# Spectral filter and gated feed-forward on one core: the constant-term column's products in a bank of their own, and three small moves around it

## The chip, the cores and the metric

The kernel runs on one core of a Trainium2 chip. The metric is device time in microseconds for one execution. The profile is one execution, recorded by the hardware profiler; its span runs from the first to the last instruction.

The core has five engines that run side by side and wait for each other by semaphores: TensorE (PE; its weight loads are listed apart as PEld), VectorE (DVE), ScalarE (ACT), GpSimd (POOL) and SyncE (SP), which here only issues DMAs. Each engine runs its own instructions in the order in which the program gives them.

## What is computed

The reference, cut to what matters (`x` is 8192 tokens of 448 channels; `sa`, `ca`, `ga`, `sb`, `cb`, `gb` are six rows made from a condition vector):

```python
h = layernorm(x) * (1 + ca) + sa
Xf = rfft2(h, axes=(tokens))                 # complex, per channel
z = Xf.reshape(..., 4, 112)                  # four blocks of channels
hr = relu(zr @ w1[0] - zi @ w1[1] + b1[0])
hi = relu(zi @ w1[0] + zr @ w1[1] + b1[1])
or_ = softshrink(hr @ w2[0] - hi @ w2[1] + b2[0], 0.01)
oi_ = softshrink(hi @ w2[0] + hr @ w2[1] + b2[1], 0.01)
x = x + ga * irfft2(or_ + 1j * oi_)
h = layernorm(x) * (1 + cb) + sb
x = x + gb * ((gelu(h @ w_gate) * (h @ w_up)) @ w_down)
```

All the edits lie in the first half, the spectral filter.

## The kernel before

**Stages.** The Fourier transform over 8192 tokens is split into two: a first transform over 128 (`dft_a`, with the layer norm's scales folded into its matrix), written to DRAM (`td`), and a second over 64 with the twiddles in its matrices. Then follow the complex two-layer perceptron per frequency, the inverse of the second transform (`stage_i1`), a store to DRAM (`vd`), and, in the second half of the kernel, the inverse of the first. After that the feed-forward part runs over 32 chunks of 256 tokens, and takes the rest of the time; nothing of the change is in it.

**Units and steps.** The frequencies are worked on in 32 units: 16 groups `bt` of four first-transform frequencies, times two halves `h` of the channels (two blocks of 112 each, `kk` 0 and 1). The order of the groups is 1, 2, 3, 4, 0, 5, ..., so the two units of group 0 are units 8 and 9. `step(i)` is a software pipeline written out by hand. In this order it

- fetches unit i+2 from `td` (`fetch_t`, L417, on SP's queue),
- runs the second transform of unit i (`stage_s2`): products L449, L450 and L455 into two banks tagged `pa`, then per block a cast on ScalarE (`zh`, L461) and a residual on VectorE (`zl`, L462),
- splits unit i+1 into a high and a low part (`split_t`: L115 and L117, on POOL; for the first two units on ScalarE and VectorE),
- runs the second layer of unit i-2 (`stage_m2`): products L522 to L529 into a bank tagged `pc`, twice (`p` 0 and 1); ScalarE's L538 and four VectorE instructions L546 apply the threshold and write `y`,
- runs the first layer of unit i-1 (`stage_m1`): 12 products per block (L494 to L501) into a bank tagged `pb`, then ScalarE's `hh` (L508) and VectorE's `hl` (L509),
- splits `y` (`yh` on ScalarE, `yl` on POOL), and
- runs the inverse of unit i-3 (`stage_i1`): L575 to L577 into two banks tagged `pd`, copied out by ScalarE as `us` (L579) and stored.

Each tag has two banks, used in turn: a tile waits until the last reader of the tile before the last has finished. The `pd` banks also serve the weight norms (`pw`, L809, emptied by VectorE's L816) and, for group 0, `pn`.

Between these stages `step` calls hooks (`"load"`, `"pe"`, `"pool"`, `"act"`, `"dve"`), to which `at(i, hook, fn)` pins other work, such as weight norms (`squares` L798 or L800, `norms` L809), sums of the third weight (L937 to L941) and its maxima (L925). A list `tiny` holds small instructions; each call of `drip()` (two in a transform, four in a second layer, two in a first layer) issues the next one. `VL` and `SL` put VectorE and ScalarE instructions on this list.

**The constant term.** The frequency 0 of group 0 and the Nyquist frequency are both real, and share one complex column (column 0). For group 0, `stage_s2` therefore copies the imaginary part of column 0, the Nyquist value, to an extra column (L470) and clears what has to be zero (L468, L469, L471), on POOL. `stage_m1` runs the first layer on two extra columns: 12 more products of two columns per block, behind the 12 main ones, into columns 448 and up of the bank that the second layer of the same step has just used (`last["pm2"]`). Column 0 then gets its constant from VectorE (L512 to L514). `stage_m2` runs the second layer for the extra columns (`pn`), and VectorE's L555 and L557 add the result to `y`.

**The start.** Before step 0 the modulation columns and rows are computed and folded into the first layer's weights. The two halves of `wt`, one per layer, lie in one tile of the pool `lp`, which is closed before the steps begin. The second layer's weights are scaled by `col2`, cast (`weights2_hi`: ScalarE's L320), and their residual and the negated copies made (`weights2_lo`: VectorE's L324 twice, POOL's L328 and L329 twice each). `row_copy` copies two rows (`sb_r`, `cb_r`) out of two `pd` banks.

**Row scales.** At the end of step 13 `row_scales` puts on the list `tiny`: two maxima on VectorE, four small VectorE instructions that make the scale `sk`, and two ScalarE instructions that scale `sb_r` and `cb_r` by it (all shown at L604).

Of the kernel before, what the change touches and what calls it, by code (L numbers as in the profile page):

```python
# [10 lines left out]
F32 = mybir.dt.float32  # L11
# [39 lines left out]
def spectral_geglu(ctx, tc, x, w1, b1, w2, b2, wg, wu, wd, cvec, wmod, cf1, cs2, cmi, cgm, out):  # L51
# [92 lines left out]
    with ExitStack() as actx:  # L144
# [8 lines left out]
        wt = lp.tile([113, 2, 2, NBLK, BS], F32, name="wt")  # L153
# [104 lines left out]
        col2 = lp.tile([113, 1], F32, name="col2")  # L258
# [9 lines left out]
        def dc_cols():  # L268

            ps = bank("pc", "psd")  # L270
            for r in range(2):
                for k in range(NBLK):
                    T.matmul(ps[:112, 4 * r + k : 4 * r + k + 1], wt[:112, 0, r, k, :], sa0[:, k : k + 1], start=True, stop=True)
            return lambda: V.tensor_scalar(hb, ps[:112, : 2 * NBLK], wsc[:112, 0:1], None, op0=ALU.mult)
# [22 lines left out]
        def modulated():  # L297
            V.tensor_tensor(
                w1m, wt[:, 0], ca1.rearrange("p (r k o) -> p r k o", r=1, o=1).to_broadcast([113, 2, NBLK, BS]), ALU.mult
# [17 lines left out]
        def weights2_hi():  # L317
            V.tensor_tensor(col2, col2, wsc[:113, 1:2], ALU.mult)
            wr = wt[:, 1].rearrange("p r k o -> p k r o")
            S.activation(wv[0][:, 0], wr, AF.Copy, scale=col2)  # L320

        def weights2_lo():
            for r in range(2):
                V.scalar_tensor_tensor(  # L324
                    wv[1][:, 0, :, r], wt[:, 1, r], col2, wv[0][:, 0, :, r], op0=ALU.mult, op1=ALU.subtract
# [12 lines left out]
        def load_mlp():  # L338
            for l, (w, b) in enumerate(((w1, b1), (w2, b2))):
                for r in range(2):  # L340
                    dma(wt[:112, l, r], w[r].rearrange("k i o -> i k o"))
                    dma(wt[112:113, l, r], b[r : r + 1])
            dma(mi, cmi)

        def mlp_bounds():
# [3 lines left out]
            for l in range(2):  # L349
                V.tensor_reduce(  # L350
                    wmx[:, l : l + 1], wt[:, l].rearrange("p r k o -> p (r k o)"), mybir.AxisListType.X, ALU.max, apply_absolute_value=True
# [55 lines left out]
    with ExitStack() as bctx:  # L407
# [31 lines left out]
        def stage_s2(h, bt):  # L439
# [11 lines left out]
            for kk in range(2):  # L451
# [13 lines left out]
                if bt == 0:  # L465

                    for z in (zhi, zlo):
                        G.memset(z[:BS, 0, ZW - 1 : ZW], 0.0)  # L468
                        G.memset(z[:BS, 1, ZW - 2 : ZW], 0.0)  # L469
# [6 lines left out]
        last = {}  # L476

        def stage_m1(h, bt):
            zs = ctx_u.pop(("z", h, bt))
            hs = []  # L480
            w = GB * 64
            for kk in range(2):
                k = 2 * h + kk
                zhi, zlo = zs[kk]
                ps = bank("pb", "pm1")
                outs = [(ps[:BS, : 2 * w], 0, w)]
                if bt == 0:
                    outs.append((last["pm2"][:BS, D + 4 * kk : D + 4 * kk + 4], w, 2))
                for e, c0, n in outs:
                    q = slice(c0, c0 + n)  # L490
                    o = [e[:, ro * n : (ro + 1) * n] for ro in range(2)]
                    for ro in range(2):
                        a, c = (0, 2) if ro == 0 else (1, 0)
                        T.matmul(o[ro], w1h[:113, a, k, :], zhi[:113, 0, q], start=ro == 0, stop=False)  # L494
                        T.matmul(o[ro], w1l[:113, a, k, :], zhi[:113, 0, q], start=False, stop=False)  # L495
                        T.matmul(o[ro], w1h[:BS, c, k, :], zhi[:BS, 1, q], start=False, stop=False)  # L496
                        T.matmul(o[ro], w1l[:BS, c, k, :], zhi[:BS, 1, q], start=False, stop=False)  # L497
                    for ro in range(2):
                        a, c = (0, 2) if ro == 0 else (1, 0)
                        T.matmul(o[ro], w1h[:BS, a, k, :], zlo[:, 0, q], start=False, stop=False)  # L500
                        T.matmul(o[ro], w1h[:BS, c, k, :], zlo[:, 1, q], start=False, stop=ro == 1)  # L501
                hhi = hh_[cnt["h"] % 4]
                cnt["h"] += 1
                hlo = bp.tile([BS, 2, ZW], F16, tag="hl", name="hl", bufs=4)
                for e, c0, n in outs:
                    q = slice(c0, c0 + n)
                    pv = e.rearrange("p (r q) -> p r q", r=2)
# [1528 lines left out]
```

## Time and profile before

| | |
|---|---|
| time, median of 3 runs | 1875.99 us (1871.98 to 1878.42) |
| the profiled execution | 1877.36 us, span 1875.3 us |
| TensorE matmuls busy | 1830.7 us, 98% of the span, 23400 instructions |
| VectorE busy | 1410.3 us, 75% |
| ScalarE busy | 973.3 us, 52% |
| GpSimd busy | 1313.4 us, 70% |
| mean granted TensorE clock | 0.987 of full |
| the steps of the spectral filter | from 79 us on; units 8 and 9 pass their first layers in the steps begun at 141.45 and about 156 us |

A row of a timeline gives the start in us from the span's start, the duration, the engine, the line of the kernel, the operation, output and inputs by name, and in brackets how long the engine stood idle before it and what ended the wait. Rows that belong together are merged (x2 is two instructions). A matmul's end is modelled, and matmuls overlap, so that their spacing is read from their starts. A window gives the busy time of each engine in a stretch, the TensorE clock that was granted (1.00 is full, 0.50 half), the mean share of the DMA engines' time in use, and GB/s moved.

### The profile page before, as it was taken

The numbers are of one execution on the slowest core, as the hardware profiler recorded it, in microseconds if no ns is written. First come the engines' busy times: TensorE is split into PE (matmuls) and PEld (weight loads), VectorE is DVE, ScalarE is ACT, GpSimd is POOL, SyncE is SP. The second block draws the span as 40 slices with busy tenths as digits, with TensorE's granted clock in tenths as the row PEclk, the third lists the DMA queues.
The fourth block names the chain that finished last, engine by engine and source line by source line (L and its number), as shares of the span: only waits on it lengthen the run. The fifth ranks groups of instructions, "written<-read, shape, count | busy, mean of one in ns | idle before, by whom it ended". The sixth has DMA issues, their size and how long they took to land.

```text
span 1875.3 us, 56506 instructions
## 1 busy us (share of the span) xinstructions
PE 1830.7 (98%) x23400; PEld 1737.4 (93%) x23400; DVE 1410.3 (75%) x2898; ACT 973.3 (52%) x1821; POOL 1313.4 (70%) x1721
## 2 busy tenths in 40 slices
PE   7999999899999999999999999999999999999998
PEld 3698889778899898999999999999999999999998
DVE  8786899887766667777777777777777777777745
ACT  5675678653444444455555555555555554444443
POOL 3475778347777778777777777777777777777534
PEclk9997999999999999999999999999999999999999
DMA  9887767664444445966666666666666676666661
GB/s 354 302 288 232 220 193 224 195 175 100 117 104 103 104 88 124 304 170 171 169 170 169 169 169 169 170 171 177 177 176 170 173 178 176 176 174 177 152 164 55
DMA packets 380089, 330.48 MB, mean 176 GB/s; under 512 B 110260, under 2 KB 358200, under 8 KB 379832
## 3 DMA queue, kind: packets, MB, share of 16 engines
q1 hardware_dynamic: 379832, 326.87, 63.2%
q8 instruction: 183, 3.00, 0.7%
q14 instruction: 74, 0.61, 0.1%
HBM read 243.32 MB, written 60.10 MB: 162 GB/s over the span
## 4 chain that ended last, share of the span: by engine, by line
PE 87%; DVE 5%; DMA 4%; ACT 2%; SPq 1%; issue 1%; POOL 1%; ACTq 0%; DVEq 0%; POOLq 0%
PE set L1471 39%; PE pgu L1228 10%; PE pdn L1301 6%; PE pdn L1303 6%; PE pdn L1302 6%; PE set L1302 2%; PE set L1303 2%; PE set L1301 2%; PE ps L213 2%; DMA xt<-in_A_x 2%; DVE y L546 1%; PE pm L494 1%; PE pm L496 1%; PE pm L495 1%; PE pm L497 1%
## 5 line engine op out<-in xcount | busy, mean ns | idle before, releaser
L1471 PE MATMUL set<-nt,wk 128*128 128x128 f16 x13104 | 736.6, 219 | 2.2 <-DMA wk<-wk 1.0
L1471 PEld LDWEIGHTS <-wk 128*128 128x128 f16 x13104 | 733.9, 98 | 2.8 <-issue 1.6
L1303 PE MATMUL pdn<-wd,ac 128*128 128x224 f16 x1218 | 315.5, 259 | 0.6 <-DVE ac L1289 0.6
L1301 PE MATMUL pdn<-wd,ac 128*128 128x224 f16 x1218 | 315.7, 259 | 0.0
L1302 PE MATMUL pdn<-wd,ac 128*128 128x224 f16 x1218 | 315.5, 259 | 0.0
L1228 PE MATMUL pgu<-nt,wk 128*128 128x256 f16 (+1 forms) x2464 | 268.0, 273 | 3.2 <-DVE x L1269 3.1
L1228 PEld LDWEIGHTS <-wk 128*128 128x128 f16 (+1 forms) x2464 | 225.6, 98 | 44.3 <-issue 18.7
L1520 ACT ACTIVATE gl<-c,dg 128x384 f32<-128x384 f32 x168 | 103.5, 616 | 230.6 <-DVE c L1514 227.7
L1546 DVE SCALAR_TENSOR_TENSOR ac<-x,sa_act,ac 128x896 f16<-128x896 f32 x168 | 206.3, 1228 | 20.2 <-ACT ac L1536 20.2
L1277 POOL TENSOR_TENSOR x<-x 128x128 f32<-128x128 f32 x223 | 131.6, 590 | 118.1 <-DVE x L1269 57.5
L1347 POOL TENSOR_TENSOR cq<-cq 128x224 f32<-128x224 f32 x32 | 21.1, 659 | 261.7 <-DVE cq L1346 261.7
L1278 POOL TENSOR_TENSOR x<-x 128x128 f32<-128x128 f32 x223 | 185.0, 830 | 17.5
L1536 ACT ACTIVATE ac<-x,sa_act 128x896 f16<-128x896 f32 x168 | 174.2, 1037 | 14.5 <-POOL x L1280 7.8
L1524 DVE TENSOR_TENSOR x<-c,gl 128x384 f32<-128x384 f32 x168 | 153.2, 912 | 17.2 <-ACT gl L1520 17.1
L1301 PEld LDWEIGHTS <-ac 128*128 128x128 f16 x1568 | 153.4, 98 | 4.9 <-issue 4.8
L1303 PEld LDWEIGHTS <-ac 128*128 128x128 f16 x1568 | 153.4, 98 | 0.8 <-DVE ac L1289 0.8
L1302 PEld LDWEIGHTS <-ac 128*128 128x128 f16 x1568 | 153.5, 98 | 0.1
L1508 DVE TENSOR_TENSOR c<-set,sb 128x512 f32<-128x512 f32 x168 | 115.4, 687 | 36.1 <-PE set L1471 36.0
L117 POOL TENSOR_TENSOR yl<-y,yh 128x448 fp32r<-128x448 f32 x63 | 87.2, 1400 | 68.7 <-ACT yh L115 51.0
L1279 POOL TENSOR_TENSOR x<-x 128x128 f32<-128x128 f32 x223 | 132.9, 596 | 0.0
L1264 ACT ACTIVATE gel<-pgu,dg 128x256 f32<-128x256 f32 x112 | 49.5, 471 | 156.9 <-PE pgu L1228 149.3
L1499 ACT COPY sb<-set 128x512 f32<-128x512 f32 x168 | 97.6, 581 | 61.3 <-PE set L1471 60.0
(330 smaller groups left out, 3869.1 us busy)
## 6 DMA issues: line engine op xcount, KB each, us to landing
wk<-wk SPq DMA_DIRECT2D x76, 1024.0 KB, 8.9
wk<-wk SPq DMA_DIRECT2D x76, 768.0 KB, 5.1
tr<-td SPq DMA_DIRECT2D x32, 448.0 KB, 4.8
vd<-us SPq DMA_DIRECT2D x64, 224.0 KB, 3.2
xx<-in_A_x SPq DMA_DIRECT2D x32, 448.0 KB, 4.8
v<-vd SPq DMA_DIRECT2D x63, 224.0 KB, 5.6
out<-x SPq DMA_DIRECT2D x31, 448.0 KB, 6.4
xt<-in_A_x SPq DMA_DIRECT2D x15, 896.0 KB, 14.8
```

The source lines that it names most:

```text
L1228: T.matmul(pgu[i, t, q][:, pr * H : (pr + 1) * H], ws[rows, n, w, tw], nts[i][rows, tn, :], start=start, stop=stop, skip_group_check=True,)
L1277: e.tensor_tensor(s1, a21, a22, ALU.add)
L1278: e.tensor_tensor(s2, s1, a11, ALU.subtract)
L1279: e.tensor_tensor(s3, a11, a21, ALU.subtract)
L1301: T.matmul(ps, ac[:, 0, ka], w[:, 0, kb], start=n == 0, stop=False)
L1302: T.matmul(ps, ac[:, 0, ka], w[:, 1, kb], start=False, stop=False)
L1303: T.matmul(ps, ac[:, 1, ka], w[:, 0, kb], start=False, stop=n == NP - 1)
L1471: T.matmul(ps2[:, pr, reg * 128 : reg * 128 + 128], slot[:, pr, hl, wt, :], nt[:, xt, :], start=start and j == 0, stop=j == len(terms) - 1 ...
L1508: V.tensor_tensor(c[:, :, 1:3, :], p[:, :, 0:256].rearrange("p g (r c) -> p g r c", r=2), b[:, :, 0:128].rearrange("p g (o c) -> p g o c", ...
L1524: V.tensor_tensor(xs[u][:, 1::3, :], cts.pop(u)[:, 1], gls.pop(u), ALU.mult)
L1536: S.activation(ac[:, 0], xs[u][:, 0:7], AF.Copy, scale=sa_act[:, t : t + 1])
L1546: V.scalar_tensor_tensor(ac[:, 1], xs.pop(u)[:, 0:7], sa_act[:, t : t + 1], ac[:, 0], op0=ALU.mult, op1=ALU.subtract)
```

## The change

- For group 0, `stage_m1` takes one extra column instead of two. Its real and imaginary outputs need six products per block (the imaginary input is zero), 12 per unit. They are issued ahead of both blocks' main products, into a bank of their own tagged `pd`; their two casts and two residuals are issued before the main products' too.
- `stage_s2` no longer clears the extra columns (L468 and L469 go); the second layer for the extra column runs for one column.
- `weights2_hi` and `weights2_lo` are no longer called before step 0. They run in step 1's `"act"` hook: behind the transform of unit 1 and the split of unit 2, ahead of the first layer of unit 0. To live that long, the second layer's raw weights and `col2` move to the pool `mpool`.
- `row_copy(0)` comes ahead of the first two splits, `row_copy(1)` behind them.
- In `row_scales` six empty entries stand on the list between the scale `sk` and the two ScalarE scalings.

```diff
-        wt = lp.tile([113, 2, 2, NBLK, BS], F32, name="wt")
+        wt = [pool.tile([113, 2, NBLK, BS], F32, name=f"wt{l}") for l, pool in enumerate((lp, mpool))]
...
-        col2 = lp.tile([113, 1], F32, name="col2")
+        col2 = mpool.tile([113, 1], F32, name="col2")
...
                     for z in (zhi, zlo):
-                        G.memset(z[:BS, 0, ZW - 1 : ZW], 0.0)
-                        G.memset(z[:BS, 1, ZW - 2 : ZW], 0.0)
                         G.tensor_copy(z[:BS, 0, ZW - 2 : ZW - 1], z[:BS, 1, 0:1])
                         G.memset(z[:BS, 1, 0:1], 0.0)
...
         def stage_m1(h, bt):
             zs = ctx_u.pop(("z", h, bt))
-            hs = []
+            hs = [(hh_[(cnt["h"] + kk) % 4], bp.tile([BS, 2, ZW], F16, tag="hl", name="hl", bufs=4)) for kk in range(2)]
+            cnt["h"] += 2
             w = GB * 64
+
+            def out(kk, e, q):
+                pv = e.rearrange("p (r q) -> p r q", r=2)
+                hhi, hlo = hs[kk]
+                S.activation(hhi[:BS, :, q], pv, AF.Relu)
+                V.scalar_tensor_tensor(hlo[:, :, q], pv, 0.0, hhi[:BS, :, q], op0=ALU.max, op1=ALU.subtract)
+
+            if bt == 0:
+                q = slice(w, w + 1)
+                ps = bank("pd", "pmx")
+                es = [ps[:BS, 2 * kk : 2 * kk + 2] for kk in range(2)]
+                for kk in range(2):
+                    k = 2 * h + kk
+                    zhi, zlo = zs[kk]
+                    for ro in range(2):
+                        o = es[kk][:, ro : ro + 1]
+                        T.matmul(o, w1h[:113, ro, k, :], zhi[:113, 0, q], start=True, stop=False)
+                        T.matmul(o, w1l[:113, ro, k, :], zhi[:113, 0, q], start=False, stop=False)
+                        T.matmul(o, w1h[:BS, ro, k, :], zlo[:, 0, q], start=False, stop=True)
+                for kk in range(2):
+                    out(kk, es[kk], q)
...
-                if bt == 0:
-                    outs.append((last["pm2"][:BS, D + 4 * kk : D + 4 * kk + 4], w, 2))
...
-                mlp2([pn[:2, kk * BS : (kk + 1) * BS] for kk in range(2)], hs, h, slice(ZW - 2, ZW), slice(0, BS))
+                mlp2([pn[:1, kk * BS : (kk + 1) * BS] for kk in range(2)], hs, h, slice(ZW - 2, ZW - 1), slice(0, BS))
...
+        row_copy(0)
         for u in units[:2]:
             split_t(*u, el=V)
-        weights2_hi()
-        for h in range(2):
-            row_copy(h)
-        weights2_lo()
+        row_copy(1)
...
             pow2(sk, bnd, 13)
+            tiny.extend([free] * 6)
             for r in (sb_r, cb_r):
                 SL.activation(r, r, AF.Copy, scale=sk)
...
-        at(1, "act", thresholds)
+        for fn in (weights2_hi, weights2_lo, thresholds):
+            at(1, "act", fn)
```

57 lines of the change are left out of this document (23 added, 34 removed).

## Prediction

> **What bounds the kernel now.** I read the page, then the windows view on one 3.41 us grid, then the timelines of each engine around the odd windows. On the page the granted clock is full except in a few early slices; after the first fifth nothing is left to the edits, since none of their lines runs there.
>
> ```profile
> PEclk9997999999999999999999999999999999999999
> ```
>
> The grid shows why the early slices dip. Columns: stretch, length, TensorE busy us (matmuls), granted clock, DMA share, GB/s.
>
> ```profile
> 145.69:149.10 3.41, 1.27 (x13) 0.98 1.02 381
> 149.10:152.52 3.42, 3.42 (x24) 0.50 1.05 327
> 162.76:166.17 3.41, 1.11 (x12) 0.98 1.07 373
> 207.13:210.54 3.41, 1.25 (x23) 0.98 0.70 220
> 210.54:213.96 3.42, 2.33 (x20) 0.50 0.26 53
> 394.86:398.28 3.42, 2.34 (x22) 1.00 0.17 36
> 398.28:401.69 3.41, 3.41 (x34) 1.00 1.17 232
> ```
>
> A window with TensorE busy for 1.27 us or less is followed by half clock; one with 2.34 us at full clock is not. So a gap costs twice: itself, and half of each slow window (1.7 us). My threshold for what follows is between 1.27 and 2.34 us busy.
>
> The next rows are TensorE's: start, duration, line, and in brackets idle time and releaser. L449 opens a step's second transform, so its first rows mark the steps; I number a step by the unit that it transforms.
>
> ```profile
> 83.66 0.22 PE L449 MATMUL ps<-s,th 128*112 128x128 f16 x1 [2.95 <-DVE zl L462]
> 90.98 0.26 PE L525 MATMUL pm<-w2l,hh 112*128 112x224 f16 x1
> 133.75 0.22 PE L449 MATMUL ps<-s,th 128*112 128x128 f16 x1
> 141.45 0.22 PE L449 MATMUL ps<-s,th 128*112 128x128 f16 x1
> 148.92 0.21 PE L494 MATMUL pm<-zh,w1h 113*112 113x2 f16 x1 [2.14 <-DVE y L546]
> 149.94 0.23 PE L501 MATMUL pm<-zl,w1h 112*112 112x2 f16 x1
> 160.30 0.21 PE L522 MATMUL pn<-w2h,hh 113*2 113x112 f16 x1
> 160.84 0.21 PE L529 MATMUL pn<-w2h,hl 112*2 112x112 f16 x1
> 183.08 0.22 PE L449 MATMUL ps<-s,th 128*112 128x128 f16 x1
> 206.88 0.22 PE L449 MATMUL ps<-s,th 128*112 128x128 f16 x1
> 211.63 0.35 PE L809 MATMUL pw<-onesb,sq 128*128 128x1 bf16 x8 [3.25 <-ACT us L579]
> 220.60 0.22 PE L449 MATMUL ps<-s,th 128*112 128x128 f16 x1
> ```
>
> An ordinary step (8) lasts 141.45 - 133.75 = 7.70 us, and TensorE never idles in it: it is the bound. Steps 9, 10 and 11, which hold the extra column, last 183.08 - 141.45 = 41.63 us where three ordinary ones make 23.1: 18.5 us over. The step begun at 206.88 lasts 13.72 us, 6.0 over. These two places and the gap before 83.66 are where the edits act; each lies on TensorE's path.
>
> **The change, part by part.** *Extra column.* Today its products wait 2.14 us for VectorE to empty a second-layer bank (L546), and run at half clock, spaced (149.94 - 148.92)/11 = 0.093 us. Now there are 12 per unit in place of 24, ahead of the main ones, in a bank whose earlier user is long done. VectorE's rows say what then limits the three steps:
>
> ```profile
> 141.20 1.29 DVE L509 SCALAR_TENSOR_TENSOR hl<-pm,hh 112x512 f16<-112x512 f32 x2
> 143.39 1.29 DVE L462 SCALAR_TENSOR_TENSOR zl<-ps,zh 112x512 f16<-112x512 f32 x2 [0.91 <-ACT zh L461]
> 145.15 3.72 DVE L546 SCALAR_TENSOR_TENSOR y<-pm,lam,t 64x224 f32<-64x224 f32 x8 [0.40 <-POOL zh L471]
> 150.49 0.15 DVE L512 TENSOR_TENSOR h<-pm,hb 112x2 f32<-112x2 f32 x1
> 150.88 0.17 DVE L514 SCALAR_TENSOR_TENSOR hl<-h,hh 112x2 f16<-112x2 f32 x1
> 154.67 1.09 DVE L925 TENSOR_REDUCE dn<-xt 128x2 f32<-128x896 f32 x1
> 163.09 0.50 DVE L555 TENSOR_SCALAR tn<-pn,lam 2x224 f32<-2x224 f32 x1
> 163.62 0.38 DVE L557 TENSOR_TENSOR y<-pn,tn 1x224 f32<-1x224 f32 x1
> ```
>
> TensorE alone: 23.1 + 24 small products + two sets of pn products, each set (160.84 - 160.30) x 12/11 = 0.6 us. A small product lies between 0.05 (pn's spacing, at full clock) and 0.093; I take 0.05, as the clock should stay up: 23.1 + 1.2 + 1.2 = 25.5 us (26.5 at 0.093). VectorE alone, without any wait: 1.29 + 1.29 + 3.72 + 1.09 = 7.4 in each step; four chains L512 to L514 of 0.6 (150.49 to 151.05, rounded up), four small residuals of 0.15 (as L512) and two pn evictions of 0.95 (163.09 to 164.0, rounded up) add 4.9: 27.1 us. The truth lies between 25.5 and 27.1; VectorE begins with the slack of 0.91 + 0.40 in its rows but waits for ScalarE in every step, so I take 26.6, near its end. Gain 41.6 - 26.6 = 15.0 us. What is late next: the second inverse product of step 10 shares its bank with the small column, whose residual stands on VectorE behind the eight L546, so TensorE waits there about 1 us; it is inside the 26.6. One window falling below the threshold in these steps would cost 1.7, two adjoining ones 3.4. The POOL fills dropped (eight of about 0.04 us a unit) are hidden under TensorE's work and count as nothing; were POOL the bound, they would add 0.3.
>
> The Trainium skill (TensorE: Matmul & The Clock Gate, section LDWEIGHTS) prices a weight load at its columns over 1.2 GHz, 93 ns for 112 columns, whatever the clock. That is the measured spacing, yet the measured one is at half clock; by the page the term is 2.2 instead of 1.2 us, and the estimate would be 1 us longer. At full clock no row here shows this form.
>
> *Six empty places in the drip list.* Two scalings of sb_r and cb_r come to ScalarE six drips later.
>
> ```profile
> 206.46 1.84 DVE L546 SCALAR_TENSOR_TENSOR y<-pm,lam,t 64x224 f32<-64x224 f32 x4
> 208.52 0.67 ACT L604 ACTIVATE sb_r<-sb_r,sk 128x448 f32<-128x448 f32 x1 [3.06 <-DVE sk L604]
> 210.13 1.02 ACT L115 CAST yh<-y 128x448 fp32r<-128x448 f32 x2
> ```
>
> Now ScalarE blocks 3.06 us on sk, which VectorE computes behind L546; queued behind it are the second first-layer eviction, the yh casts and the us copies, and TensorE's L809 needs a bank of those copies. Without the block the casts still need VectorE's last L546, done at 208.3. From the first cast to TensorE's restart took 211.63 - 210.13 = 1.5 us with both casts; one of 0.51 remains after 208.3, so restart at 209.3: 2.3 us won. The half clock from 210.54 to about 217.4 (5.7 us of work) is gone if the window keeps 3.41 - 1.1 = 2.3 us busy, just what stayed at full clock above: 2.9 more, 5.2 in all. Against it, the two scalings (0.67 each) now lie in the next step ahead of its evictions and delay a bank there by about 1. Net 4.0, between 2 (the clock falls) and 5.
>
> *Second layer's weights.* Their ScalarE cast and VectorE residual no longer stand ahead of the first zl; they follow step 1's transform, and four POOL instructions with them.
>
> ```profile
> 80.35 1.04 ACT L320 ACTIVATE w2h<-wt,col 113x896 f16<-113x896 f32 x1 [1.23 <-DVE col L318]
> 81.42 1.58 DVE L324 SCALAR_TENSOR_TENSOR w2l<-wt,col,w2h 113x448 f16<-113x448 f32 x2 [1.11 <-ACT w2h L320]
> 81.47 1.83 POOL L328 TENSOR_SCALAR w2h<-w2h 112x448 f16<-112x448 f16 x1 [2.76 <-ACT w2h L320]
> 85.05 0.55 POOL L329 COPY w2l<-w2l 112x448 f16<-112x448 f16 x1
> 86.57 1.88 POOL L117 TENSOR_TENSOR tl<-tr,th 128x896 f16<-128x896 f32 x1
> 73.24 6.29 SPq L417 DMA_DIRECT2D tr<-td  x3
> DMA to landing us min/median/max: 3.8/3.8/3.8
> ```
>
> Step 0's transform ends at 83.66 - 2.95 = 80.7; the next then waits only for one cast and one residual, each about half of 1.29, and starts near 82.0 instead of 83.66. That is not the gain: the second layer of unit 0 needs all four POOL results, and these now stand behind unit 2's split. Its fetch is the third L417, issued about 0.4 before 79.53, landing near 82.9; the split takes 88.45 - 85.60 = 2.85 (cast and L117), so POOL is free near 85.8. The weight cast is done by about 86.1 (zl, the column of scales, 1.04), and POOL's four then take 85.60 - 81.47 = 4.1: 90.0 to 90.2. The product that reads the last of them (L525) starts at 90.98 today: 0.9 us won. But TensorE, ahead by now, runs dry from about 87.3 (first layer of unit 0 and transform 2 done) to 90.0, so some window keeps under 1.3 us busy, and the half clock costs 1.7 where everything behind is TensorE's: net -0.8. Bounds: +0.9 if the windows split the gap evenly (each then 2.0 busy), and -3.5 if the fetch lands only at 85.6, the start of unit 2's split today, which shows no wait for it (2.7 later). SyncE gains nothing and loses nothing on the path: the fetch for unit 4, which waits for unit 2's split, goes out earlier, that for unit 5 about 1 us later, a step ahead of its use. Moving row 0's copy ahead of the splits puts it into ScalarE's wait for the first fetch, and counts as nothing; uncovered it would be 0.5.
>
> *DMA.* Steps 9 to 11 become short, and the transfers must fit.
>
> ```profile
> 106.00:145.69 39.69, 39.69 (x444) 38.96 (x443) 33.94 (x70) 31.21 (x57) 30.86 (x59) 1.00 0.96 320
> 106.00:183.24 77.24, 72.79 (x720) 69.98 (x719) 55.94 (x125) 47.74 (x88) 48.59 (x77) 0.87 0.85 280
> ```
>
> (The last two columns are share and GB/s.) From 106 on 280 x 77.24 = 21.6 MB move up to step 12. At 320/0.96 = 333 GB/s they need 64.9 us; the new schedule leaves 77.24 - 15.0 = 62.2. So up to 2.7 us of transfers run late into steps 12 and 13. Loads are issued a step ahead, which covers most of it; I charge 1.0 (0 to 2.7).
>
> *Sum.* 15.0 + 4.0 - 0.8 - 1.0 = 17.2 us, and all behind is TensorE-bound and shifts whole. The profiled execution took 1877.36 us (span 1875.3 and 2.1 around it): 1860.2. The median of the runs, 1875.99 (1871.98 to 1878.42), lies 1.4 lower: 1858.8, say **1859**.
>
> **Rivals.**
> - *The clock falls again.* VectorE's lag in steps 10 to 12, or the 1.1 us gap at the drip, leaves a window under the threshold. For it: each term above ends near 2.3 us busy, and small products may count as idle (149.10:152.52 holds only full-size work behind 0.9 us of them and was not freed). Against: no gap of over 1.2 us is left there. Two or three windows of 1.7: 1862 to 1864.
> - *No half clock at the second layer of unit 0.* The gap of 2.7 us falls across two windows, or is too short: 1.7 us better, 1857. The Trainium skill (TensorE: Matmul & The Clock Gate, section Why this matters for your kernels) lets gaps up to about 3 us pass. Against it, the gap of 2.14 us above, in a window with 1.27 us busy, was followed by half clock.
> - *The wait is replaced.* The small residuals and chains stay in VectorE's order; if TensorE then stops on the shared bank for 2 us or more in both units, the clock falls as now, and of the 15.0 only the 24 products dropped are won (24 x 0.093 = 2.2), and nothing is lost to DMA: 2.2 + 4.0 - 0.8 = 5.4, 1870.6. Against: the bank wait comes out at 1 us in one step only.
> - *DMA becomes the bound (slower).* The share stands at 0.96 before step 9 already. If every step from 9 to 16 waited for a load so long that a window kept under the threshold (a wait of over 3.41 - 2.34 = 1.1 us decides), each would lose some 1.6 and 1.7 of half clock: 8 x 3.3 = 26 against 18.2 won without the DMA term: 8 us slower, 1884. Against: over the whole stretch to 183.24 the share is 0.85, and the transfers that run late have later steps to end in.
>
> **How the numbers follow.** Forecast (1855 to 1861) 0.60; clock falls again 0.17; no half clock 0.13; wait replaced 0.07; DMA 0.03. A measurement of this kernel tells about 0.3% from no change, 5.6 us, so faster is below 1870.4: the first three and about half of the fourth, 0.93; same 0.04, slower 0.03. The range takes in the bounds: 15.0 may be 16.1, 4.0 be 5.2 and -0.8 be +0.9 with no DMA loss, 22.2 in all or 1853.8, which the scatter of the runs takes to 1852. On the other side stands the clock rival's 1864 with the rest of the DMA bound (1.7) and the late fetch (2.7), 1869; beyond that lie only the last two rivals.
>
> **What would show it.** Right: the first small product follows the last second-layer product of its step without idle time; steps 9, 10, 11 last about 8.3, 9 and 9.3 us at full clock; step 15 lasts about 9; ScalarE's scaling shows no wait on sk; L809 of step 15 waits about 1 us for the copies. At the start the second transform begins near 82, POOL runs unit 2's split ahead of the four weight instructions, and the second layer of unit 0 shows a gap of 2 to 3 us on POOL, then a half-clock window. Wrong: a half-clock window in steps 9 to 16, steps 12 and 13 longer than 8 us with waits on loads, or a small product spaced at 0.09 at full clock.

## The result and the profile after

| | before | after |
|---|---|---|
| median of the runs | 1876.82 us (1869.65 to 1878.42, 6 runs) | 1864.72 us (1863.09 to 1866.30, 6 runs) |
| ratio after to before, 95% interval | | 0.9944 [0.9925, 0.9962] |
| the profiled execution | 1877.36 us, span 1875.3 | 1863.71 us, span 1861.9 |

The kernel became 12.1 us faster by the medians and 13.65 us faster by the two profiled executions (the span went down 13.4). Forecast were 1859 us, a range of 1852 to 1869, and a gain of 17.2 us. So the direction is right and the time lies in the range, but the gain is smaller than the sum, by some 3.5 us in the profiled executions and 5.1 us in the medians.

The page of the profile after: span, TensorE's busy time, and the granted clock in 40 slices.

```profile
span 1861.9 us, 56443 instructions
PE 1822.2 (98%) x23376; PEld 1726.4 (93%) x23376; DVE 1411.5 (76%) x2898; ACT 972.1 (52%) x1821; POOL 1310.9 (70%) x1705
PEclk9999999999999999999999999999999999999999
```

The dip that stood in the fourth clock slice is gone. A slice covers 46.5 us, so that one half-clock window of 3.4 us still reads as 9: the kernel after has one from 91 to 94.4 us. TensorE's timeline of the kernel after shows what the prediction told the reader to look for (L449 again opens a step's second transform; L495 to L497 are the small products, L529 to L532 the second layer, L581 the inverse, L814 the norms):

```profile
82.33 0.22 PE L449 MATMUL ps<-s,th 128*112 128x128 f16 x1 [1.25 <-DVE zl L462]
88.59 0.26 PE L530 MATMUL pm<-w2l,hh 113*128 113x224 f16 x1 [0.53 <-DVE w2l L324]
89.39 0.26 PE L531 MATMUL pm<-w2h,hh 112*128 112x224 f16 x1 [0.54 <-POOL w2h L329]
91.18 0.34 PE L532 MATMUL pm<-w2l,hh 112*128 112x224 f16 x1 [1.54 <-POOL w2l L329]
143.24 0.22 PE L449 MATMUL ps<-s,th 128*112 128x128 f16 x1
147.00 0.26 PE L536 MATMUL pm<-w2h,hl 112*128 112x224 f16 x1
147.09 0.17 PE L495 MATMUL pmx<-zh,w1h 113*112 113x1 f16 x1
147.64 0.19 PE L497 MATMUL pmx<-zl,w1h 112*112 112x1 f16 x1
152.11 0.22 PE L449 MATMUL ps<-s,th 128*112 128x128 f16 x1
162.65 0.44 PE L581 MATMUL pi<-yh,mih 128*128 128x448 f32 x1 [1.01 <-DVE hl L484]
163.33 0.22 PE L449 MATMUL ps<-s,th 128*112 128x128 f16 x1
173.04 0.22 PE L449 MATMUL ps<-s,th 128*112 128x128 f16 x1
200.96 0.34 PE L814 MATMUL pw<-onesb,sq 128*128 128x1 bf16 x8 [1.76 <-ACT us L585]
207.32 0.22 PE L449 MATMUL ps<-s,th 128*112 128x128 f16 x1
```

Three things are to be seen. The first small product (147.09) follows the last second-layer product with no idle time, and the twelve are spaced (147.64 - 147.09)/11 = 0.05 us. Steps 9 to 11 last 173.04 - 143.24 = 29.80 us instead of 41.63; one by one they last 8.87, 11.22 and 9.71 us where the prediction had about 8.3, 9 and 9.3, so that step 10 carries most of the miss. And the second layer of unit 0 runs dry three times up to 91.18, 2.6 us in all, where the prediction had TensorE dry from about 87.3 to 90.0.

Where the 13.65 us came from, by the starts of the steps in both traces:

| place | before | after | gain | forecast |
|---|---|---|---|---|
| step 0 to step 3 (the second layer's weights) | 16.44 | 17.83 | -1.4 | -0.8 |
| steps 9 to 11 (extra column) | 41.63 | 29.80 | 11.8 | 15.0 |
| steps 12 to 14 (forecast: late transfers) | 23.80 | 24.65 | -0.85 | -1.0 |
| step 15 (empty places) | 13.72 | 9.63 | 4.1 | 4.0, steps 16 and 17 included |
| steps 16 and 17 | 16.11 | 15.74 | 0.4 | |
| start of step 0 (row copies around the splits) | 79.20 | 79.58 | -0.4 | 0 |

One term carries most of the error, the extra column. The waits view of TensorE for steps 9 to 11 (waiting tile and line, the engine and line waited for: total us, times, longest) and the windows view of the same stretch say what took the place of the old limit. Before:

```profile
PE pm L494 <- DVE y L546: 4.4, 2, 2.3
141.45:183.08 41.63, 37.18 (x334) 35.10 (x333) 24.77 (x62) 19.54 (x39) 21.71 (x37) 0.75 0.76 246
```

After:

```profile
PE pm L529 <- DVE hh L521: 1.4, 2, 0.7
PE pi L581 <- DVE hl L484: 1.3, 2, 1.0
143.24:173.04 29.80, 27.00 (x310) 24.63 (x309) 26.55 (x60) 17.54 (x37) 21.22 (x29) 1.00 1.00 327
```

The clock rose from 0.75 to 1.00 and the wait for L546 is gone. In its place stand 2.7 us of new waits, all for VectorE: for the small column's residual (L484) and for column 0's constant (L521).

### The profile page after: what moved, and what is told of

The parts are those of the page before. It is cut to its first block, busy times and chain, and to the rows that moved or that the text cites. A ratio compares the mean times of both kernels' runs of the same rounds, so it can differ in the third digit from the quotient of the medians.

```text
span 1861.9 us, 56443 instructions
## 1 busy us (share of the span) xinstructions
PE 1822.2 (98%) x23376; PEld 1726.4 (93%) x23376; DVE 1411.5 (76%) x2898; ACT 972.1 (52%) x1821; POOL 1310.9 (70%) x1705
## 4 chain that ended last, share of the span: by engine, by line
PE 85%; DVE 6%; DMA 3%; POOL 2%; ACT 2%; issue 1%; SPq 1%; DVEq 0%; ACTq 0%; POOLq 0%
PE set L1477 39%; PE pgu L1234 10%; PE pdn L1307 6%; PE pdn L1309 6%; PE pdn L1308 6%; PE ps L213 2%; PE set L1307 2%; PE set L1309 2%; PE set L1308 2%; DMA xt<-in_B_w_up 1%; DVE y L552 1%; PE set L1601 1%; DVE st L174 1%; PE set L1602 0%; PE set L1603 0%
## 5 line engine op out<-in xcount | busy, mean ns | idle before, releaser
L1283 POOL TENSOR_TENSOR x<-x 128x128 f32<-128x128 f32 x223 | 131.2, 588 | 120.1 <-DVE x L1275 58.5
L1284 POOL TENSOR_TENSOR x<-x 128x128 f32<-128x128 f32 x223 | 186.0, 834 | 17.5
L1530 DVE TENSOR_TENSOR x<-c,gl 128x384 f32<-128x384 f32 x168 | 153.4, 913 | 17.2 <-ACT gl L1526 17.1
L1285 POOL TENSOR_TENSOR x<-x 128x128 f32<-128x128 f32 x223 | 132.2, 593 | 0.0
L1286 POOL TENSOR_TENSOR x<-x 128x128 f32<-128x128 f32 x223 | 126.3, 566 | 0.0
```

The source lines that it names most:

```text
L1283: e.tensor_tensor(s1, a21, a22, ALU.add)
L1284: e.tensor_tensor(s2, s1, a11, ALU.subtract)
L1285: e.tensor_tensor(s3, a11, a21, ALU.subtract)
L1286: e.tensor_tensor(s4, a12, s2, ALU.subtract)
L1530: V.tensor_tensor(xs[u][:, 1::3, :], cts.pop(u)[:, 1], gls.pop(u), ALU.mult)
```

## The experiments

Two explanations for the 3.2 us missing in steps 9 to 11 were set against each other. *VectorE's order:* evictions of the new bank and the chain for column 0 take longer than their own durations, and TensorE waits for them. *DMA:* the loads cannot keep up with the shorter steps. A third question was whether each edit gives what its term said, alone.

**1. The three edits one at a time, on one chip.** The kernel before took 1873.97 us there (24 runs). Each of the first three kernels is the kernel before with one of the edits (the first keeps the second layer's raw weights and `col2` in `mpool`); the fourth is the kernel after with the calls of `weights2_hi`, `weights2_lo` and `row_copy` put back ahead of step 0.

> The kernel before with the extra column's edit alone (12 small products ahead, in a bank of their own). Theory A: each edit acts in its own place and the places add. Then steps 9 to 11 last 29.8 us as in the changed kernel, against 41.6 before, step 15 keeps its 13.7, and the time falls by 11.8 us, to about 1865. Rival B: the places depend on each other (what one frees, a later load or the clock takes back, or the other two edits make the room for it). Then steps 9 to 11 are not near 29.8, or the time falls by under 9 or over 14 us.

> The kernel before with the second layer's weights moved behind the two transforms (and the row copies parted around the splits) alone. Theory A: slower by 1.8 us, what step 3 starts later in the changed kernel (97.41 against 95.64): the fourth second-layer product of unit 0 waits for POOL to about 91, and a half-clock window follows. 1878 to 1879. Rival B: the 1.8 us are chance (where the clock's windows fall, when the first fetch lands): 1876 to 1877, or faster, with no half-clock window near 91.

> The kernel before with the six empty places alone. Theory A: step 15 lasts 9.6 us instead of 13.7, no half clock at 210, and the steps behind it are 0.4 us shorter in all: 4.5 us less, about 1872. Rival B: without the column's edit the list falls on other steps' work and the gain is under 2 us or, with the clock, over 6.

> The changed kernel with the weights and the row copies put back to where they were. Theory A: the start costs nothing any more, step 3 starts near 95.6 and the time is 1.8 us under the changed kernel's 1864.7: about 1863. Rival B: the half clock falls somewhere else, or the shortened start runs into late loads by step 9: no faster than 1864.7.

| kernel | median us | ratio to before | 0 to 3 | 9 to 11 | 12 to 14 | 15 |
|---|---|---|---|---|---|---|
| column alone | 1867.06 | 0.9954 [0.9934, 0.9974] | 13.60 | 29.80 | 24.65 | 11.12 |
| weights alone | 1876.92 | 1.0013 [0.9994, 1.0032] | 18.43 | 37.00 | 23.78 | 12.78 |
| empty places alone | 1868.47 | 0.9957 [0.9941, 0.9974] | 13.25 | 41.45 | 23.79 | 8.92 |
| after without the weights' move | 1865.49 | 0.9946 [0.9928, 0.9964] | 16.83 | 30.45 | 24.66 | 9.21 |

(The last four columns are step lengths of the profiled executions.) The gain belongs to the column and the empty places: alone they give 6.9 and 5.5 us by the medians. Moving the weights gives nothing that these runs show (the interval holds 1), and without the move the kernel cannot be told from the kernel after (0.9946 and 0.9944); the expected loss of 1.8 us is neither shown nor excluded. The column's 6.9 us are fewer than the 11.8 expected, and fewer than the 9 under which its rival would hold, but its interval, 4.9 to 12.4 us, takes in both. Whether the two gains add is open as well: together (fourth row) they give 8.5 us, and their sum would be 12.4. Steps 9 to 11 last 29.8 and steps 12 to 14 24.65 with the column alone: both come from this edit, whatever the others do.

The rows also show the limits of single profiles. With the column alone, TensorE still stalls about 3.26 us at the norms of step 15, yet the step lasts 11.12 us and not 13.72, since no half-clock window followed this time. With the weights alone, steps 9 to 11 last 37.0 and not 41.6, with nothing in them changed. A gap near the threshold costs itself each time and half clock only when the 3.41 us grid falls badly. And the profiled executions of the first and the fourth kernel (1861.91 and 1860.95 us) were the fastest of their runs, some 5 us under the medians: the step lengths say where time went, not how much the runs won.

**2. Both small casts ahead of both small residuals.** In the kernel after, cast, residual, cast, residual alternate between ScalarE and VectorE on one bank.

```diff
-                for kk in range(2):
-                    out(kk, es[kk], q)
+                for kk in range(2):
+                    S.activation(hs[kk][0][:BS, :, q], es[kk].rearrange("p (r q) -> p r q", r=2), AF.Relu)
+                for kk in range(2):
+                    V.scalar_tensor_tensor(hs[kk][1][:, :, q], es[kk].rearrange("p (r q) -> p r q", r=2), 0.0, hs[kk][0][:BS, :, q], op0=ALU.max, op1=ALU.subtract)
```

> The changed kernel, with both blocks' casts of the small column issued ahead of both residuals, where cast, residual, cast, residual stood. Theory C: in steps 9 to 11 VectorE is the bound, and part of its time is spent on waits for ScalarE around the shared bank (0.24 and 0.31 us in each unit: the second small cast waited 0.56 and 1.29 us for the first small residual, and the main residual then for the main cast). Then steps 9 to 11 fall from 29.8 to about 28.7 to 29.2 us. Rival D: late transfers bind these steps (ScalarE waited 1.23 us for a load in step 9, POOL 0.41 in step 10): they stay at 29.8.

Measured: 1863.83 us, 0.9941 [0.9917, 0.9964]; steps 9 to 11 28.76 us, steps 12 to 14 24.03. The kernel after has 29.80 and, in its second profile (below), 30.49, so the gain there is 1.0 to 1.7 us. The times themselves cannot be told apart (0.9941 and 0.9944). The alternation is seen in the kernel after, in ScalarE's and VectorE's timelines around 151:

```profile
150.90 0.18 ACT L483 ACTIVATE hh<-pmx 112x2 f16<-112x2 f32 x1 [0.56 <-DVE hl L484]
151.11 0.17 DVE L484 SCALAR_TENSOR_TENSOR hl<-pmx,hh 112x2 f16<-112x2 f32 x1 [0.24 <-ACT hh L483]
151.59 0.69 DVE L484 SCALAR_TENSOR_TENSOR hl<-pm,hh 112x512 f16<-112x512 f32 x1 [0.31 <-ACT hh L483]
```

The second small cast, 0.18 us long, waits for the first residual, although it reads other columns; the large cast queued behind it is late by as much. Pairing takes this away. The waits of TensorE in these steps fall from 2.7 to 1.4 us:

```profile
PE pi L583 <- DVE hl L501: 0.9, 1, 0.9
PE pm L531 <- DVE hh L523: 0.5, 1, 0.5
```

**3. The DMA rival.** The late stores of the first transform are issued earlier, in steps 0 to 8 (the list gives how many per step):

```diff
-        for i, n in enumerate([3, 4, 4, 4, 5, 5, 2, 2, 2, 2, 3]):
+        for i, n in enumerate([5, 5, 5, 5, 5, 5, 2, 2, 2]):
```

> The changed kernel, with the late stores of the first transform issued in steps 0 to 8 instead of 0 to 10, more of them in the first five steps, so that steps 9 and 10 issue none. Rival D: with about 1.1 MB less to move in steps 9 and 10 the wait for a load in step 9 (1.23 us) goes, and steps 9 to 13 (46.4 us in the changed kernel, 29.8 and 16.6) fall by 1 to 3 us. Theory C: the wait may go, but steps 9 to 11 stay at 29.8, and steps 12 and 13 at 16.5.

Measured: 1867.66 us, 0.9962 [0.9945, 0.9979]. No engine waited for a load in steps 9 to 13 (in step 14 GpSimd did, for 1.06 us), and the DMA share in steps 9 to 11 was 0.85 where the kernel after has 1.00. Yet steps 9 to 11 took 30.46 us and steps 12 to 14 24.66, no less than in the kernel after. The DMA rival falls, for steps 12 to 14 too.

**4. Column 0's constant without VectorE: first try.** ScalarE adds the bias in two casts and copies the result, GpSimd forms the residual.

```diff
-                    V.tensor_tensor(h0, ps[:BS, 0 : w + 1 : w], hb[:, k : 2 * NBLK : NBLK], ALU.add)
-                    V.tensor_scalar(hhi[:BS, :, 0], h0, 0.0, None, op0=ALU.max)
-                    V.scalar_tensor_tensor(hlo[:, :, 0], h0, 0.0, hhi[:BS, :, 0], op0=ALU.max, op1=ALU.subtract)
+                    for ro in range(2):
+                        S.activation(h0[:, ro : ro + 1], ps[:BS, ro * w : ro * w + 1], AF.Relu, bias=hb[:, ro * NBLK + k : ro * NBLK + k + 1])
+                    S.copy(hhi[:BS, :, 0], h0)
+                    G.tensor_tensor(hlo[:, :, 0], h0, hhi[:BS, :, 0], ALU.subtract)
```

> The changed kernel, with column 0's constant taken off VectorE: ScalarE adds it (two casts with a bias and a copy per block), GpSimd forms the residual. Theory C: VectorE loses four chains of 0.6 us and the 3.1 us by which single small instructions were longer beside GpSimd's yl (1.15 us where 0.17 is usual), so steps 9 to 11 fall from 29.8 to 26 or 27 us, near TensorE's own 25.5, and the time by 3 to 4 us to about 1861. Rival D (late transfers bind): 29.8, and the time stays at 1864.7.

Measured: 1869.95 us, 0.9973 [0.9958, 0.9988]; steps 9 to 11 34.8 us, 5.0 longer. As a test of the chain it failed, since it brought a wait of its own. TensorE's waits view of these steps, and ScalarE's and VectorE's timelines:

```profile
PE pw L815 <- ACT us L586: 5.4, 2, 2.8
155.40 0.41 ACT L521 ACTIVATE h<-pm,hb 112x1 f32<-112x1 f32 x2 [0.76 <-DVE hl L484]
156.57 0.69 DVE L484 SCALAR_TENSOR_TENSOR hl<-pm,hh 112x512 f16<-112x512 f32 x1 [1.20 <-ACT hh L483]
```

The bias casts read the bank that VectorE's residual is reading, and wait for it; the next block's cast stands behind them, and VectorE then waits 1.20 us for that. The copies `us`, for which TensorE waits at the norms, stand behind all of it in ScalarE's order. It is the alternation of experiment 2 again, with large tiles, and a half-clock window besides.

**5. Column 0's constant on TensorE.** Experiment 2, and four products per block of the identity with a high and a low half of the bias add the constant in the bank; the chain is gone.

```diff
+                if bt == 0:
+                    for ro in range(2):
+                        j = ro * NBLK + k
+                        for hbx in (hbh, hbl):
+                            T.matmul(o[ro][:, 0:1], ident[:BS, :BS], hbx[:, j : j + 1], start=False, stop=False)
...
-                if bt == 0:
-                    h0 = bp.tile([BS, 2], F32, tag="h0", name="h0", bufs=2)
...
+        G.tensor_copy(hbh, hb)
+        G.tensor_tensor(hbl, hb, hbh, ALU.subtract)
```

> The kernel with paired small evictions (casts ahead of residuals), and column 0's constant added by TensorE: eight products of one column per unit with the identity into the main bank, so that VectorE's chain of three small instructions per block is gone. Theory C: what still keeps steps 9 to 11 at 28.8 us is VectorE, with four chains of 0.6 us and some 3 us in which chain instructions with two SBUF inputs lasted until GpSimd's yl ended (1.02 to 1.15 us where 0.17 is usual). Then steps 9 to 11 fall to 26 to 26.5, near TensorE's 25.5 to 25.9, and the time lies about 4 us under the changed kernel, near 1860.5. Rival G: with VectorE free, ScalarE or the bank of the second inverse product binds: 28 us or more.

Measured: 1860.55 us (1860.31 to 1861.74), 0.9929 [0.9914, 0.9944]. The windows view of its steps 9 to 11, and VectorE's timeline behind the eight L556 of step 9:

```profile
146.63:173.48 26.85, 26.85 (x326) 25.83 (x325) 22.83 (x50) 18.71 (x39) 21.21 (x29) 1.00 1.00 336
```

```profile
150.34 3.72 DVE L556 SCALAR_TENSOR_TENSOR y<-pm,lam,t 64x224 f32<-64x224 f32 x8 [0.40 <-ACT t L548]
154.08 0.23 DVE L503 SCALAR_TENSOR_TENSOR hl<-pmx,hh 112x2 f16<-112x2 f32 x2
```

The stretch is 26.85 us and TensorE is busy for 26.85 of it: no wait is left, with 16 more products than in the kernel after. Steps 12 to 14 are back at 23.77. The chain had cost 28.76 - 26.85 = 1.9 us beyond what the alternation cost: its own instructions and their lengthening beside GpSimd (see below) together, which this run does not part.

**6. The weights earlier.** Cast and residual of the second layer's weights go ahead of step 1's transform; GpSimd's four instructions stay behind unit 2's split.

```diff
+        def weights2_neg():
...
-        for fn in (weights2_hi, weights2_lo, thresholds):
+        for fn in (weights2_hi, weights2_lo):
+            at(1, "load", fn)
+        for fn in (weights2_neg, thresholds):
             at(1, "act", fn)
```

> The changed kernel, with the second layer's cast and residual issued ahead of step 1's transform (behind step 0's), and only GpSimd's four instructions left where the change put them, behind unit 2's split. Theory E: what makes the start late is the cast, which stands behind the second transform's evictions on VectorE and ScalarE, so that GpSimd idles 1.29 us between the split (85.7) and the weights (87.0), and the half clock that follows. Then the fourth second-layer product starts near 90 instead of 91.2, and step 3 1.3 us earlier, or 3 us if the gap gets too short for a half-clock window: 94.4 to 96.1 instead of 97.4. Rival F: it is the split ahead of the weights on GpSimd, or the fetch: step 3 stays near 97.4.

Measured: 1861.69 us, 0.9934 [0.9911, 0.9957]; step 0 to 3 14.99 us, with no half-clock window there. This length misleads. The expectation spoke of the start of step 3, and step 3 starts at 97.21, near the 97.41 of the kernel after, as its rival had it; the length is short because step 0 started late in this profile, at 82.22 instead of 79.58, behind a half-clock window that ended at 80.1. The small column of scales, which takes 0.15 us in the kernel after, took 1.78:

```profile
85.32 1.89 POOL L117 TENSOR_TENSOR tl<-tr,th 128x896 f16<-128x896 f32 x1
85.43 1.78 DVE L318 TENSOR_TENSOR col<-col,wsc 113x1 f32<-113x1 f32 x1
87.25 1.04 ACT L320 ACTIVATE w2h<-wt,col 113x896 f16<-113x896 f32 x1 [2.57 <-DVE col L318]
```

VectorE's instruction started 0.11 us after GpSimd's L117 and both ended at 87.21. So the next kernel forms that column before the first split:

```diff
         def weights2_hi():
-            V.tensor_tensor(col2, col2, wsc[:113, 1:2], ALU.mult)
...
+        V.tensor_tensor(col2, col2, wsc[:113, 1:2], ALU.mult)
         row_copy(0)
         for u in units[:2]:
```

> The kernel with the second layer's cast and residual ahead of step 1's transform, and the column of scales (one VectorE instruction with two SBUF inputs, 1.78 us in that kernel because it stood beside GpSimd's split, 0.15 elsewhere) formed before the first split. Theory H: that instruction held the cast, and so GpSimd's four, back: from step 0 to step 3 there pass 13.4 to 14.0 us instead of 15.0 (17.8 in the changed kernel), without a half-clock window at the second layer of unit 0; about 4 us under the changed kernel, 1860.5. Rival F (GpSimd's order or the fetch): 15 us again, 1862.

Measured: 1862.60 us (1861.72 to 1863.47), 0.9939 [0.9924, 0.9954]. The expected length was missed: step 0 to 3 took 17.43 us, from 79.56 to 96.99. The column now took 0.16 us and the residual was done at 84.3, yet GpSimd's four had not moved. GpSimd's and TensorE's timelines:

```profile
83.69 1.38 POOL L115 CAST th<-tr 128x896 f16<-128x896 f32 x1 [4.62 <-DMA tr<-td]
85.15 1.89 POOL L117 TENSOR_TENSOR tl<-tr,th 128x896 f16<-128x896 f32 x1
87.00 1.33 POOL L329 TENSOR_SCALAR w2h<-w2h 112x448 f16<-112x448 f16 x1
90.68 0.26 PE L533 MATMUL pm<-w2l,hh 112*128 112x224 f16 x1 [1.54 <-POOL w2l L330]
```

The fetch of unit 2 landed at 83.7 here instead of the 82.8 of the kernel after, and the split stands ahead of the four in GpSimd's order; the gap of 1.54 us and a half-clock window behind it stayed. That is the rival's account, GpSimd's order or the fetch. In the run before, TensorE reached these products only at 92.05, when GpSimd was nearly through, so that the gap had not shown. The start of step 3 gains 0.2 to 0.7 us in these two profiles (97.21 and 96.99, against 97.41 and 97.70 in the two profiles of the kernel after).

**7. All of it, and the kernel after again, on one chip.** The sum of experiments 5 and 6 (last form), beside the kernel after:

> Both of these together. Theories C and H: the gains stand at different places and add, 7 to 8 us under the changed kernel: about 1857, 0.991 of the kernel before. Rivals: one place takes back what the other gives (late loads in steps 9 to 14 with the start 4 us earlier): 1860 or more.

> The changed kernel once more, beside the others on the same chip: 0.9944 of the kernel before within 0.002, as the yardstick for the three variants.

| kernel | median us | runs | ratio to before |
|---|---|---|---|
| after | 1864.01 | 1863.32 to 1865.42 | 0.9947 [0.9932, 0.9962] |
| after, weights earlier | 1862.60 | 1861.72 to 1863.47 | 0.9939 [0.9924, 0.9954] |
| after, constant on TensorE | 1860.55 | 1860.31 to 1861.74 | 0.9929 [0.9914, 0.9944] |
| both | 1857.21 | 1856.49 to 1858.85 | 0.9911 [0.9894, 0.9928] |

The version with both is the fastest, 6.8 us below the kernel after, near the 7 to 8 expected; alone the two win 1.4 and 3.5 us, and what the further 1.9 us are is not shown. Its steps 9 to 11 last 26.86 us and steps 12 to 14 23.76. A half-clock window still follows the second layer of unit 0, from 91.5 to 94.9.

## Why the prediction was right or wrong

**What bounds the kernel: right, but busy time alone is not the threshold.** The early half-clock windows were the price of short gaps, and in the kernel after the bounds of 1.27 and 2.34 us held. Windows of the kernel after, with TensorE's busy time and the clock:

```profile
87.58:90.99 3.41, 0.99 (x10) 0.51 (x9) 3.34 (x10) 1.34 (x3) 3.41 (x4) 1.00 1.02 372
90.99:94.40 3.41, 3.22 (x18) 2.55 (x18) 1.16 (x3) 0.63 (x1) 2.90 (x3) 0.51 0.59 237
159.26:162.67 3.41, 2.40 (x21) 2.03 (x18) 2.86 (x8) 2.12 (x5) 0.20 (x1) 1.00 1.01 329
162.67:166.08 3.41, 2.75 (x39) 2.40 (x39) 3.13 (x7) 3.37 (x8) 2.28 (x3) 1.00 1.07 360
```

0.99 us busy was followed by half clock; 2.40 was not. The rival of a clock that falls again in steps 9 to 16 did not come true; of the replaced wait only the wait came, 2.7 us in four pieces too short for half clock. Not true either was the rival of no half clock at unit 0's second layer: the gaps there, 0.53, 0.54 and 1.54 us, were each far below 3 us, and the slow window came. The Trainium skill (TensorE: Matmul & The Clock Gate, section Why this matters for your kernels), which lets gaps up to about 3 us pass, is not borne out by this window: no single gap in it was long, but little of it was busy.

Other traces go beyond these bounds. In the kernel with the weights' move alone:

```profile
166.78:170.19 3.41, 2.69 (x37) 2.69 (x38) 1.91 (x7) 0.71 (x3) 0.00 (x0) 1.00 0.79 306
170.19:173.60 3.41, 3.41 (x19) 3.04 (x19) 3.22 (x6) 2.22 (x6) 2.65 (x3) 0.50 0.02 5
```

Here 2.69 us busy were followed by half clock. 24 of the 37 matmuls are products of two columns, about 1.2 us of it by their spacing, so the prediction's suspicion that small products may count as idle fits; no run tests it. And 1.79 us busy were followed by half clock in experiment 3 (88.25 to 91.67), while 1.46 were not in experiment 4 (155.23 to 158.65). The runs give no sharp limit in busy time.

**Extra column: mechanism right, size off, 15.0 forecast and 11.8 measured.** That the wait for L546 and the half clock would go is what happened. The step that failed is the sum "VectorE alone, without any wait", 27.1 us, taken as an upper bound ("The truth lies between 25.5 and 27.1"); the stretch took 29.80. It summed VectorE's durations as the trace of before showed them, and left out two things. First, the second small cast waits for VectorE's residual on the same bank, and the large cast behind it in ScalarE's order is late by as much (experiment 2, 1.0 us or more). Second, the chain's small instructions last longer beside GpSimd's `yl`, which they now meet. VectorE was busy for 26.55 of the 29.80 us. VectorE's and GpSimd's timelines of the kernel after:

```profile
152.59 1.15 DVE L522 SCALAR_TENSOR_TENSOR hl<-h,hh 112x2 f16<-112x2 f32 x1
154.86 0.17 DVE L522 SCALAR_TENSOR_TENSOR hl<-h,hh 112x2 f16<-112x2 f32 x1
163.81 1.15 DVE L522 SCALAR_TENSOR_TENSOR hl<-h,hh 112x2 f16<-112x2 f32 x1
166.09 0.83 DVE L522 SCALAR_TENSOR_TENSOR hl<-h,hh 112x2 f16<-112x2 f32 x1
152.57 2.22 POOL L117 TENSOR_TENSOR yl<-y,yh 128x448 fp32r<-128x448 f32 x2 [1.40 <-DVE hh L521]
```

The same 112x2 instruction takes 0.17 us, or 1.15 when one of the two `yl` (1.1 us each) started just ahead of it. Its four rows here hold 0.98 + 0 + 0.98 + 0.66 = 2.6 us over 0.17 each. That TensorE pays for them is seen where one of them differs by chance. In the second profile of the kernel after, the row that stands at 154.86 above reads:

```profile
155.15 0.89 DVE L522 SCALAR_TENSOR_TENSOR hl<-h,hh 112x2 f16<-112x2 f32 x1
```

Steps 9 to 11 last 30.49 us there instead of 29.80. The other profiles with this form of the column agree: 29.80 us where the row takes 0.17 us (column alone), 30.43 to 30.57 where it takes 0.83 or 0.84 (four profiles of experiments 1, 3 and 6). Removing the chains gave 1.9 us back. Take both away, and the stretch lasts 26.85 us. That this is near the 26.6 of the forecast is in part luck: the limit is then TensorE, with 16 products more, and not VectorE. Without them, at 0.05 each, TensorE alone comes to about 26.0 us, an estimate, where the prediction added up 25.5. The 1 us that TensorE was to wait for the second inverse product of step 10 measured 1.01. The small product at 0.05 us is right. The Trainium skill (TensorE: Matmul & The Clock Gate, section LDWEIGHTS) gives the time of a weight load as its columns over 1.2 and names no clock; for 112 columns that is an estimate of 93 ns. The spacing of 0.093 us at half clock agrees with it, the 0.05 at full clock does not.

**Late transfers: the number right by luck, the reason wrong.** -1.0 was forecast for steps 12 and 13, and -0.85 came in steps 12 to 14. Steps 12 and 13 last 8.39 and 8.16 us, over the 8 us that the prediction named as a sign against it, but without the waits on loads that went with it: the trace of the kernel after has none in these two steps. Experiment 3 took the loads' waits away without shortening these steps, and experiments 2 and 5, which touch no transfer, brought them to 24.03 and 23.77 us. What fits is VectorE's backlog and ScalarE's: TensorE's one wait there, 0.5 us, is for ScalarE's copies `us`.

**Empty places: right,** 4.1 + 0.4 against 4.0. ScalarE's wait on `sk` is gone and the slow window with it. The restart at L814 waits 1.76 us where 1.1 was forecast, because the last `yh` cast still waits for VectorE's last L552:

```profile
199.91 0.56 ACT L115 CAST yh<-y 128x448 fp32r<-128x448 f32 x1 [1.68 <-DVE y L552]
```

The size varies from run to run, and the traces show why. One of the small instructions that make the scale lasted until GpSimd's split ended, and VectorE's L552 stands behind it. VectorE's and GpSimd's timelines:

```profile
194.21 1.61 DVE L610 SCALAR_TENSOR_TENSOR hb<-rmax 128x1 f32<-128x1 f32 x1
193.91 1.89 POOL L117 TENSOR_TENSOR tl<-tr,th 128x896 f16<-128x896 f32 x1
```

In the second profile of the kernel after it took 0.92 us, and the wait at L814 was 1.07; in experiment 3, where it started 0.12 us before GpSimd's split, it took 0.15. In all ten profiles that have the empty places and no half-clock window in step 15, the step lasts 8.0 us plus the duration of this one instruction, 8.18 to 9.63 us in all.

**Second layer's weights: -1.4 against -0.8 in the profiles, open in the runs.** GpSimd's and ScalarE's timelines after:

```profile
82.81 0.93 POOL L115 CAST th<-tr 128x896 f16<-128x896 f32 x1 [5.42 <-DMA tr<-td]
85.88 1.04 ACT L320 ACTIVATE w2h<-wt,col 113x896 f16<-113x896 f32 x1 [0.94 <-DVE col L318]
87.00 1.82 POOL L328 TENSOR_SCALAR w2h<-w2h 112x448 f16<-112x448 f16 x1 [1.29 <-ACT w2h L320]
90.58 0.55 POOL L329 COPY w2l<-w2l 112x448 f16<-112x448 f16 x1
```

The fetch landed at 82.8 (forecast 82.9) and the transform began at 82.33 (near 82). The step that missed by a microsecond is "the weight cast is done by about 86.1": the column of scales stood behind VectorE's second `zl` (ended 85.7), the cast ended at 86.9, and GpSimd waited 1.29 us for it, so that the product begins at 91.18 and not at 90.0 to 90.2. What the move costs in all stays open. The lengths of step 0 to 3 fall into two groups, by whether step 0 starts at 79.2 to 79.6 us or, behind a half-clock window that ended at 78.0 to 80.2, at 81.0 to 82.3. With the early start they are 16.44 and 16.83 us without the move (before, and the fourth kernel of experiment 1) and 17.83 to 18.43 with the move as in the change (three profiles), 1.0 to 2.0 us worse; with the late start 13.25 and 13.60 without it and 17.82 to 19.28 with it (four profiles), 4.2 to 6.0 us worse. Yet the ratios with and without the move (0.9944 and 0.9946) cannot be told apart.

## What to carry to other kernels

When an eviction gets a bank of its own, cost it by the queues of the engines that empty it, not by its duration: two engines that read one bank by turns wait for each other, so issue all of one engine's reads, then all of the other's. Price a small VectorE instruction with two inputs in SBUF beside long GpSimd instructions at up to the rest of the GpSimd instruction; if it is on the path, give its work to an engine that has none of this (here, four tiny products on TensorE were cheaper than three tiny VectorE instructions). For gaps near the clock's threshold, sum TensorE's busy time per window, do not lean on products of one or two columns in that sum, and expect single runs to differ by where the windows fall. Set step lengths of two profiles side by side only where the first step starts alike in both.

## What the runs showed of the hardware

- A VectorE instruction of one or two columns lasted until the end of the GpSimd instruction that had started just before it: 0.15 us alone and 1.78 or 1.61 beside L117, 0.17 and 1.15 beside `yl`. Started 0.12 us before L117, it took 0.15. The Trainium skill (SBUF — State Buffer, section Who interferes with whom) says that a VectorE instruction with two SBUF inputs and a GpSimd instruction that reads SBUF exclude each other, and that the one issued second waits for the whole of the other; both ends at 87.21, and both at 195.8, agree with it.
- ScalarE's and VectorE's reads of one bank came one after the other even for different columns: waits of 0.24 us for two-column tiles, 0.76 for large ones. They are waits on semaphores, so the runs show this of the programs; whether the chip would need it was not tried.
- The same gap has two prices. The stall at the norms of step 15, 3.25 us in the kernel before and 3.26 with the column alone, made the step 13.72 us long with a half-clock window behind it, and 11.12 without.
